# Packing the half-seen key tiles of the even query blocks two to a column, in an attention stage ahead of a routed feed-forward on one Trainium2 core

## The chip, the cores and the metric

The kernel runs on one core of one Trainium2 chip. The metric is device time in microseconds (us); lower is better. Its time before is the median of three runs, 455.78 us (454.82 to 455.80). The profile comes from one further execution, whose own time is 456.63 us and whose span, from the first to the last instruction, is 454.9 us. The granted TensorE clock was 0.996 of full speed over that span.

Engines are named as in the profile: PE is TensorE (matmul), PEld its weight loads, DVE is VectorE, ACT is ScalarE, POOL is GpSimd, SP is SyncE, which here issues DMAs.

## The reference, cut to what matters

```python
# attention: 8 batches x 8 heads, 576 positions, head size 64
block_i, block_j = pos[:, None] // 64, pos[None, :] // 64
scores = np.where(block_i >= block_j, q @ k.T / sqrt(64), -1e9)
attn = softmax(scores)                 # over the keys
x = attn @ v                           # [8, 576, 512] over all heads
# then a top-1 mixture of experts: 8 experts, relu(x @ w1[e]) @ w2[e], times a probability
```

A query block of 64 positions sees all keys of its own block and of the earlier ones. There are 9 query blocks, 0 to 8. A softmax does not change when one number is subtracted from all scores of a query, whatever the number.

## The kernel before, in words

**The work.** 64 heads are taken as 32 pairs. One pass of the loop at line 973 (a *round*, `it` from -2 to 31) works on up to four pairs at once: `a = it + 2` is being transposed (its q and k come in and are turned), `c = it + 1` gets its maxima and its first score segments, `e = it` gets its last score segments and its product with V, and `x = it - 1` is normalised and written to DRAM rows for the second stage. A feed-forward stage over 128-row tiles of tokens follows after round 31. A planner (`at`, `run`) strews small routing steps over the rounds 9 to 31, mostly on DVE.

**Scores.** They stand transposed: 128 keys in the partitions, queries in the columns. Key tile `j` holds key blocks `2j` and `2j + 1`; tile 4 holds block 8 alone. Both heads of a pair lie in one PSUM tile `[128, 2, 512]`, two banks. `SEGS` (line 411) lists four *segments*, each a list of (key tile, first query, number of queries, column). Tile 0 has 576 queries, tile 1 has 448, then 320, 192 and 64: 1600 columns for each head. A segment takes three steps: `products` (line 646) multiplies K by Q in fp32, one matmul for each head, 64 rows of the array each, and each of these shows as two passes in the profile; `less` (line 654) subtracts from each query its maximum, as a bf16 matmul of ones with a diagonal that holds minus the maximum; `expo` (line 663) takes the exponential on ACT from PSUM into `prob`.

**Half-seen tiles.** Query block `2j` sees only the first half of key tile `j`. `corners` (line 671) lets POOL overwrite the other half of these 64 columns with zeros, four memsets for each pair.

**Maxima.** `top` (line 573) forms scores once more in bf16 with queries in the partitions, into a PSUM tile of the same ring, and DVE reduces them. `top` job 2 covers the low query blocks, job 1 (`mid_maxima`, line 627) the middle ones and also block 0, job 0 (`high_maxima`, line 633) the high ones. From the maxima, `low_shift` on POOL (blocks 1 to 6), the end of `high_maxima` on DVE (blocks 7 and 8) and `first_shift` on DVE (block 0, line 617, two instructions, one for each head) write the diagonals. For pair 0 they stand in `diag0`; for all the other pairs there is one tile, `diag1`, `[128, 9, 64]`, written anew for each pair. `mid_maxima(i)` calls `first_shift(i)` for `i > 1`.

**V.** `av` (line 678) multiplies `prob` (64 queries as weights, 128 keys as rows) by `vt`, V with a column of ones, 50 matmuls of 65 columns for a pair.

**The order in a round from 1 to 29** (lines 1100 to 1223), as written; the order is kept, and each engine takes its own instructions strictly in it. A wait is put in by itself wherever an instruction reads what an earlier one in the written order wrote, or overwrites what an earlier one read:

1. `norm(x)` on DVE;
2. `mid_maxima(c, 0)`: PE scores, DVE reduce, POOL exchange, `first_shift(c)` on DVE;
3. segments 3 and 2 of pair `e`;
4. `turns` and `turned_in`: PE transposes of pair `a`, ACT copies into `plb`;
5. `low_shift(c)`, `high_maxima(c, 1)`, then on POOL `halves_in` (a copy into `qh`) and one corner;
6. products of segments 0 and 1 of pair `c`; `tails` (PE transposes, ACT copies); `top(a, 2, 1)`; small POOL copies and a cast;
7. `less` and `expo` of segments 0 and 1 of pair `c`, three corners, `low_exchange(a)`;
8. `av(e, ...)` and the normalisation of its last rows.

PSUM: three tiles `s0`, `s1`, `s2` for scores and maxima, reached through `ring`, whose last two entries change places after each round, and two banks `g0`, `g1` for transposes and `av`.

Of the kernel before, what the change touches and what calls it, by code (L numbers as in the profile page):

```python
# [16 lines left out]
def kernel(  # L17
# [11 lines left out]
    nc = tc.nc  # L29
    F32 = mybir.dt.float32  # L30
# [15 lines left out]
    P = 128  # L46
# [352 lines left out]
    def slots(inv, tok_g, tok_s):  # L399
# [4 lines left out]
        if tok_s is not None:  # L404
# [13 lines left out]
    def place(j, q0):  # L418
        for s, parts in enumerate(SEGS):
# [18 lines left out]
    with tc.manual_schedule():  # L438
# [223 lines left out]

        def expo(i, ps, s):
            p = prob[i % 2]
            w = sum(x[2] for x in SEGS[s])
            nc.scalar.activation(p[:, :, SEG0[s]:SEG0[s] + w], ps[:, :, 0:w],  # L666
                                 func=AF.Exp, scale=scale_attn)
            if s < 2:
                corners(i, s)

        def corners(i, s):
            p = prob[i % 2]
            for (j, a, n, c) in SEGS[s]:
                if j < 4 and a == 128 * j:
                    cc = SEG0[s] + c
                    nc.gpsimd.memset(p[64:128, :, cc:cc + 64], 0.0)  # L676

        def av(i, g, m):
# [9 lines left out]
            for h in range(2):  # L688
                for j in range(m + 1):
                    for e in range(2):  # L690
                        c = place(j, 128 * m + 64 * e)
                        nc.tensor.matmul(g[rows(e), o + 65 * h:o + 65 * h + 65],  # L692
                                         lhsT=p[:, h, c:c + 64], rhs=t[:, j, h, :],
                                         start=(j == 0), stop=(j == m))
# [278 lines left out]
        for it in range(-2, NPR):  # L973
# [56 lines left out]
            def tails():  # L1030

                tail = nat[:, 8].rearrange("p h d -> p (h d)") if on_a else None
                if on_x:
                    if it < NPR - 2:
                        g0, g1 = gx = g_tile(0), g_tile(1)
                    else:
                        ps = seg_tile(1 if on_c else 0)
                        gx = ps[:, 0, :], ps[:, 1, :]
                        g1 = gx[1]
# [43 lines left out]
            if it == -2:  # L1083
# [5 lines left out]
                top(0, 2, 1)  # L1089
                low_exchange(0)  # L1090
                weights(2)
                mid_maxima(0, 2)
# [3 lines left out]
                products(0, opened, 0, 1)  # L1096
                high_maxima(0, 1)
# [9 lines left out]
            if it == 0:  # L1107
                segment(3, 1)
                mid_maxima(c, 0)
                turns()  # L1110
                segment(2, 2)
            elif on_e:
# [3 lines left out]
                segment(3, 1)  # L1116
                segment(2, 2)
# [18 lines left out]
            if on_e:  # L1136
                corners(e, 2)
            run(it, "begin")
            if on_c and not on_e:
                ps0, ps1 = opened, seg_tile(2)  # L1140
                for z in range(2):
                    products(c, ps1, 1, z)
                top(a, 2, 1)
            if on_c and on_e:
                ps0, ps1 = seg_tile(0), seg_tile(2)
# [3 lines left out]
                products(c, ps0, 0, 1)  # L1149
            g1 = tails()  # L1150
            if on_e and on_a:
                top(a, 2, 1)
# [12 lines left out]
            if on_c:  # L1165
                for z, ps in enumerate((ps0, ps1)):
                    less(c, ps, z, 0)
                    less(c, ps, z, 1)
# [53 lines left out]
            if on_e:  # L1222
                ring[1:] = ring[:0:-1]
# [182 lines left out]
```

## Time and profile before

| | |
|---|---|
| median of 3 runs | 455.78 us |
| the profiled execution: its own time / its span | 456.63 / 454.9 us |
| PE busy | 429.3 us, 94% of the span |
| weight loads (PEld) busy | 338.4 us, 74% |
| DVE busy | 316.4 us, 70% |
| POOL busy | 295.5 us, 65% |
| ACT busy | 271.5 us, 60% |

A row of the timeline gives the start and the length of a group in us, then engine, line, operation, what it writes and reads with the shapes, the number of instructions (x), and in square brackets how long the engine had been idle before and what ended the wait. For a matmul the first shape is rows times columns of the array that it uses, the second rows times moving columns. A round begins with the PE rows of line 583.

### The profile page before, as it was taken

Reading aid. Unit: us, or ns where it says so; the run is one execution under the profiler, and the core shown is the slowest. Engines: PE = TensorE matmul, PEld = TensorE weight load, DVE = VectorE, ACT = ScalarE, POOL = GpSimd, SP = SyncE. Lnnn points to the kernel's source line nnn. Section 1 sums busy time; section 2 is a strip of 40 time slices with the busy share of each in tenths; the row PEclk is TensorE's granted clock in tenths of the full one; section 3 lists DMA queues with packets and bytes.
Section 4 is the critical chain, followed back from the end, with each engine's and each line's share of the span. In section 5 each row is a group of like instructions: output and inputs, shape, how many; then the busy total and the mean of one; then the engine's idle time right before and its main releaser. Section 6 shows DMA issues by size and latency. Waiting matters only on the chain. (4 is left out here: it accounts for less than half of the span.)

```text
span 454.9 us, 19769 instructions
## 1 busy us (share of the span) xinstructions
PE 429.3 (94%) x7780; PEld 338.4 (74%) x7802; DVE 316.4 (70%) x843; ACT 271.5 (60%) x573; POOL 295.5 (65%) x700
## 2 busy tenths in 40 slices
PE   7899899999999999899999999999999999999994
PEld 5688688878787877788778887786776676766772
DVE  4777667768778788887899998866865873333322
ACT  3856666766567757775777576454554553553552
POOL 4556466657556666887566788654877767667652
PEclk8999999999999999999999999999999999999999
DMA  7999799899999987999889998857545545555551
GB/s 153 187 164 173 138 177 184 157 186 171 184 171 171 170 167 149 194 157 180 172 167 178 163 192 145 143 107 161 139 131 154 143 124 155 146 123 156 138 122 66
DMA packets 169887, 71.18 MB, mean 156 GB/s; under 512 B 151424, under 2 KB 158080, under 8 KB 169792
## 3 DMA queue, kind: packets, MB, share of 16 engines
q1 hardware_dynamic: 154640, 38.05, 43.3%
q0 software_dynamic: 13952, 31.52, 34.4%
q8 instruction: 65, 1.06, 1.0%
q10 hardware_dynamic: 1200, 0.30, 0.3%
q14 instruction: 30, 0.25, 0.2%
HBM read 67.18 MB, written 14.97 MB: 181 GB/s over the span
## 5 line engine op out<-in xcount | busy, mean ns | idle before, releaser
L666 ACT ACTIVATE prob<-ps_s 128x640 f32<-128x640 f32 (+2 forms) x128 | 103.7, 839 | 44.1 <-PE ps_s L659 42.9
L594 DVE TENSOR_REDUCE mx<-ps_m 128x2 f32<-128x640 f32 (+2 forms) x96 | 100.3, 1044 | 17.5 <-PE ps_m L589 6.4
L650 PE MATMUL ps_s<-plb 64*128 64x320 f32 (+4 forms) x768 | 104.9, 394 | 1.2 <-DVE mx L597 0.9
L650 PEld LDWEIGHTS ps_s<-plb 64*128 64x128 f32 x768 | 69.2, 188 | 22.5 <-issue 11.1
L692 PE MATMUL g<-vt,prob 128*64 128x65 f32 x2560 | 81.1, 222 | 0.5 <-issue 0.4
L692 PEld LDWEIGHTS g<-vt,prob 128*64 128x64 f32 x2560 | 77.9, 138 | 1.0 <-issue 0.9
L827 ACT ACTIVATE hT<-ps_h 128x512 bf16<-128x512 f32 x76 | 43.9, 596 | 42.5 <-PE ps_h L823 28.4
L838 PE MATMUL ps_o<-w_bf,hT 128*128 x282 | 67.1, 379 | 1.4 <-issue 0.3
L838 PEld LDWEIGHTS <-hT 128*128 128x128 bf16 x304 | 28.0, 98 | 27.9 <-issue 0.3
L804 DVE COPY natb<-w_bf 128x4096 bf16 x20 | 24.7, 1236 | 30.9 <-PE ps_h L823 23.7
L841 ACT ACTIVATE o_sb<-ps_o,share 128x512 f32<-128x512 f32 x37 | 25.4, 687 | 29.5 <-PE ps_o L838 12.0
L804 DVE COPY plb<-w_bf 128x4096 bf16 x20 | 24.7, 1234 | 23.3 <-PE ps_h L823 13.7
L823 PEld LDWEIGHTS <-plb 128*128 128x128 bf16 x608 | 35.4, 98 | 7.0 <-issue 2.9
L823 PEld LDWEIGHTS <-natb 128*128 128x128 bf16 x608 | 35.4, 98 | 7.0 <-issue 2.3
L659 PE MATMUL ps_s<-diag,ones 64*128 64x448 bf16 (+1 forms) x372 | 36.7, 274 | 1.1 <-DVE diag L613 0.6
L63 POOL DMA_DIRECT2D w_bf<-in_moe_w_dram x56 | 34.1, 608 | 1.5 <-DMA x_rows<-xb 0.4
L1023 ACT COPY plb<-g 128x512 f32<-128x512 f32 x62 | 33.2, 593 | 1.2 <-PE g L987 1.2
L607 POOL COPY mx<-mx 64x2 f32<-64x2 f32 x64 | 11.7, 183 | 33.7 <-DVE mx L594 32.2
L676 POOL MEMSET prob<- 64x128 f32 x128 | 24.3, 205 | 13.1 <-ACT prob L666 7.6
L847 POOL DMA_INDIRECT out_dram<-o_sb,tok2s x17 | 19.0, 1117 | 20.0 <-ACT o_sb L841 10.9
L568 PE MATMUL ps_m<-kh,qh 64*128 64x320 bf16 (+2 forms) x192 | 25.7, 309 | 3.3 <-POOL qh L1028 1.2
L684 PEld LDWEIGHTS g<-vt,prob 128*64 128x64 f32 x640 | 21.4, 137 | 9.7 <-ACT xT L720 4.6
(291 smaller groups left out, 803.7 us busy)
## 6 DMA issues: line engine op xcount, KB each, us to landing
w_bf<-in_moe_w_dram POOLq DMA_DIRECT2D x48, 256.0 KB
vt<-in_v_dram SPq DMA_DIRECT2D x64, 128.0 KB
natb<-in_k_dram SPq DMA_DIRECT2D x63, 128.0 KB
natb<-in_q_dram SPq DMA_DIRECT2D x63, 128.0 KB
w_bf<-in_moe_w_dram POOLq DMA_DIRECT2D x8, 512.0 KB
x_rows<-w_bf SPq DMA_DIRECT2D x13, 256.0 KB
natb<-in_k_dram SPq DMA_DIRECT2D x32, 32.0 KB
vt<-in_v_dram SPq DMA_DIRECT2D x32, 32.0 KB
```

The source lines that it names most:

```text
L63: nc.gpsimd.dma_start(out=dst[:, e * WE:(e + 1) * WE].rearrange("p (k f) -> p k f", k=n)[:, r:r + m, :], in_=view[e][:, r:r + m, :])
L568: nc.tensor.matmul(ps[:, h, c:c + w], lhsT=qh[rows(h), 64 * b:64 * b + 128], rhs=kh[rows(h), 0:w], start=True, stop=m is None)
L594: nc.vector.reduce_max(mx[:, 7:12:4] if job == 0 else mx[:, b:b + 2], ps[:, :, 0:w], axis=AX)
L650: nc.tensor.matmul(ps[:, h, c:c + n], lhsT=pls[i][rows(h), S + 128 * j:S + 128 * j + 128], rhs=pls[i][rows(h), a:a + n], start=part == 0, ...
L659: nc.tensor.matmul(ps[:, h, c:c + n], lhsT=ones[rows(h), :], rhs=diag[rows(h), a // 64:(a + n) // 64, :], start=False, stop=part == len(SE ...
L666: nc.scalar.activation(p[:, :, SEG0[s]:SEG0[s] + w], ps[:, :, 0:w], func=AF.Exp, scale=scale_attn)
L692: nc.tensor.matmul(g[rows(e), o + 65 * h:o + 65 * h + 65], lhsT=p[:, h, c:c + 64], rhs=t[:, j, h, :], start=(j == 0), stop=(j == m))
L804: nc.vector.tensor_copy(w, w1_bf[:, bass.ds(off, WE)])
L823: nc.tensor.matmul(ps_h[:, f, :], lhsT=w[:, f0 + ko * F:f0 + ko * F + 2 * P - 1:2], rhs=xb[:, ko * P:(ko + 1) * P], start=(ko == 0), stop= ...
L827: nc.scalar.activation(hT[:, half * 4:half * 4 + 4, :], ps_h, func=AF.Relu)
L838: nc.tensor.matmul(ps_o, lhsT=hT[:, fo, :], rhs=w2_bf[:, bass.ds(woff + fo * Dm, Dm)], start=(fo == 0), stop=(fo == FO - 1))
L1023: nc.scalar.copy(pl[:, w * S:w * S + 512], pw[w])
```

## The change: what it does, and the diff

The half-seen tiles leave `SEGS`. Each of the four even blocks 0, 2, 4, 6 now has its own 64-key by 64-query piece, and two pieces share 64 columns: blocks 0 and 4 in one place (block 0 in partitions 0 to 63, block 4 in 64 to 127), blocks 2 and 6 in another. There are 1472 columns for each head, in three segments of 512, 512 and 448; the last one holds all four pieces. `products_halves` and `less_halves` make the pieces with matmuls of 64 rows by 64 columns of the array. The corners go; instead POOL copies the half of V that belongs to each piece into `vh`, a tile whose other half stays zero (`halves_v`, two copies for each pair), and `av` takes `vh` for the diagonal tile of an even block. The last segment of `e` is made in one go at step 3, with `s1`; maxima of steps 5 and 6 go to `s2`, segment 1 of pair `c` to `s1`, and the ring stays as it is after round 0.

```diff
-    SEGS = [[(1, 128, 448, 0), (4, 512, 64, 448)],
-            [(0, 0, 256, 0), (3, 384, 192, 256)],
-            [(2, 256, 320, 0)],
-            [(0, 256, 320, 0)]]
-    SEG0 = [448, 0, 960, 1280]
-    WP = 1600
+    SEGS = [[(0, 64, 512, 0)],
+            [(1, 192, 384, 0), (3, 448, 128, 384)],
+            [(2, 320, 256, 0), (4, 512, 64, 384)]]
+    HALVES = [(0, 0, 256), (4, 1, 256), (2, 0, 320), (6, 1, 320)]
+    SEG0 = [0, 512, 1024]
+    WP = 1472
...
+        vh = const([P, 4, 2, D + 1], F32, "vh")
+        nc.gpsimd.memset(vh, 0.0)
+        for z in range(2):
+            nc.gpsimd.memset(vh[64 * z:64 * z + 64, 2 * z:2 * z + 2, :, D:D + 1], 1.0)
...
+        def products_halves(i, ps):
+            for b, z, c in HALVES:
+                for h in range(2):
+                    nc.tensor.matmul(ps[rows(z), h, c:c + 64],
+                                     lhsT=pls[i][rows(h), S + 64 * b:S + 64 * b + 64],
+                                     rhs=pls[i][rows(h), 64 * b:64 * b + 64],
+                                     start=False, stop=False)
+
+        def less_halves(i, ps):
+            diag = diag1 if i else diag0
+            for b, z, c in HALVES:
+                for h in range(2):
+                    nc.tensor.matmul(ps[rows(z), h, c:c + 64], lhsT=ones[rows(h), 0:64],
+                                     rhs=diag[rows(h), b, :], start=False, stop=False)
...
-        def corners(i, s):
...
+        def halves_v(i):
+            for z in range(2):
+                nc.gpsimd.tensor_copy(vh[rows(z), 2 * z:2 * z + 2, :, 0:D],
+                                      vt[i % 2][rows(0), 2 * z:2 * z + 2, :, 0:D])
...
-                                         lhsT=p[:, h, c:c + 64], rhs=t[:, j, h, :],
+                                         lhsT=p[:, h, c:c + 64],
+                                         rhs=(t if e or j < m else vh)[:, j, h, :],
...
-            def segment(s, where):
+            def segment(where):
                 ps = seg_tile(where)
-                products(e, ps, s, 0)
-                less(e, ps, s, 0)
-                expo(e, ps, s)
+                for z in range(2):
+                    products(e, ps, 2, z)
+                products_halves(e, ps)
+                less_halves(e, ps)
+                for z in range(2):
+                    less(e, ps, 2, z)
+                expo(e, ps, 2)
...
                 if on_c:
                     mid_maxima(c, 0)
                 run(it, "mid")
-                segment(3, 1)
-                segment(2, 2)
+                segment(1)
                 if on_a:
                     turns()
...
-                    high_maxima(c, 1)
+                    high_maxima(c, 2)
...
-                corners(e, 2)
+                halves_v(e)
...
-                ps0, ps1 = seg_tile(0), seg_tile(2)
+                ps0, ps1 = seg_tile(0), seg_tile(1)
...
-                top(a, 2, 1)
+                top(a, 2, 2)
```

On PE, at step 3 of a round in the middle of the stage, before the change: two segments of pair `e`, products (line 650) and subtraction (line 659) of each, with no wait but the first. `ps_s` is the score tile, `plb` holds q and k, `diag` the diagonals.

```order
L650 MATMUL ps_s<-plb 128x320 [waits Activation_49]
L650 MATMUL ps_s<-plb 128x320
L659 LDWEIGHTS ones
L659 MATMUL ps_s<-diag,ones 128x320
L659 LDWEIGHTS ones
L659 MATMUL ps_s<-diag,ones 128x320
L650 MATMUL ps_s<-plb 128x320 x2
L659 LDWEIGHTS ones
L659 MATMUL ps_s<-diag,ones 128x320
L659 LDWEIGHTS ones
L659 MATMUL ps_s<-diag,ones 128x320
```

On PE at the same place now (line 657 is `products`, 673 `products_halves`, 682 `less_halves`):

```order
L657 MATMUL ps_s<-plb 128x256 [waits Activation_49]
L657 MATMUL ps_s<-plb 128x256
L657 MATMUL ps_s<-plb 128x64 x2
L673 MATMUL ps_s<-plb 64x64 x8
L682 LDWEIGHTS ones
L682 MATMUL ps_s<-diag,ones 64x64 [waits DVE_49]
L682 LDWEIGHTS ones
L682 MATMUL ps_s<-diag,ones 64x64 [waits DVE_49]
L682 LDWEIGHTS ones
L682 MATMUL ps_s<-diag,ones 64x64
```

One segment stands where two stood, eight small products and eight small subtractions are in it, and the first two subtractions, those of block 0, carry a wait for DVE each. In the built program the two counts that they wait for are those of the two instructions of line 627 (`first_shift`) that DVE runs for pair `c` in the same round.

On POOL, from step 5 to step 6, before (613 is `low_shift`, 1028 `halves_in`, 676 a corner, 1068 to 1072 `tails_in`):

```order
L613 TENSOR_TENSOR diag<-negi,mx 128x384 [waits PE_49,Pool_49]
L1028 CAST qh<-plb 128x512 [waits PE_49,Activation_49]
L676 MEMSET prob_148 64x2x64 [waits Pool_49]
L1068 CAST kh<-plb 128x64 [waits Activation_49,Pool_49]
L1069 CAST qh<-plb 128x64 [waits Activation_49]
L1072 CAST qh<-plb 128x2x64
```

On POOL at the same place now:

```order
L620 TENSOR_TENSOR diag<-negi,mx 128x384 [waits PE_49,Pool_49]
L1051 CAST qh<-plb 128x512 [waits PE_49,Activation_49]
L693 COPY vh<-vt_149 64x4x64 [waits DMAHW5_49,DMAHW4_49]
L693 COPY vh<-vt_149 64x4x64 [waits Pool_49]
L1091 CAST kh<-plb 128x64 [waits Activation_49,Pool_49]
L1092 CAST qh<-plb 128x64 [waits Activation_49]
L1095 CAST qh<-plb 128x2x64
```

Two copies stand where one memset stood; the other three memsets, later in the round between the cast and `low_exchange`, are gone.

More of the change, by code (lines that the diff above doesn't have):

```diff
@@ L1036, in tails @@
                     else:
[L1037 removed]
+                        ps = seg_tile(2 if on_c else 0)
                         gx = ps[:, 0, :], ps[:, 1, :]
@@ L1088 @@
                 load_ends(2)
-                top(0, 2, 1)
+                top(0, 2, 2)
                 low_exchange(0)
                 weights(2)
-                mid_maxima(0, 2)
+                mid_maxima(0, 1)
                 low_shift(0)
@@ L1095 @@
                 products(0, opened, 0, 0)
-                products(0, opened, 0, 1)
-                high_maxima(0, 1)
+                high_maxima(0, 2)
                 continue
@@ L1107 @@
             if it == 0:
-                segment(3, 1)
+                segment(2)
                 mid_maxima(c, 0)
                 turns()
-                segment(2, 2)
+                ring[1:] = ring[:0:-1]
             elif on_e:
@@ L1148 @@
                     products(c, ps1, 1, z)
-                products(c, ps0, 0, 1)
             g1 = tails()
             if on_e and on_a:
-                top(a, 2, 1)
+                top(a, 2, 2)
             if on_a:
@@ L1166 @@
                 for z, ps in enumerate((ps0, ps1)):
-                    less(c, ps, z, 0)
-                    less(c, ps, z, 1)
+                    for y in range(len(SEGS[z])):
+                        less(c, ps, z, y)
                     expo(c, ps, z)
```

18 lines of the change are left out of this document (5 added, 13 removed).

## The prediction

> **What bounds the kernel now.** I read the page first (PE busy in 94% of the span), then the busy time by windows, then the timeline of one whole round with all engines, and last the same few rows of every other round. The windows, with the length in us, then busy time of PE, PEld, DVE, ACT and POOL, then granted clock, DMA share and GB/s:
>
> ```profile
> 23.53:280.26 256.73, 248.53 (x5419) 204.50 (x5416) 206.76 (x557) 172.69 (x393) 171.79 (x536) 1.00 0.93 169
> 49.47:61.09 11.62, 10.28 (x220) 7.96 (x217) 7.46 (x20) 6.05 (x13) 7.38 (x25) 1.00 0.65 132
> 78.12:86.63 8.51, 8.41 (x188) 7.03 (x185) 6.32 (x16) 5.94 (x13) 5.36 (x17) 1.00 0.87 147
> ```
>
> The rounds 1 to 28 take 256.73 us and PE works in 248.53 of them. The third row is round 7, a plain one: 8.41 of 8.51 us. So the attention stage is bound by PE's instruction stream; whatever lengthens that stream or halts it is paid at once. The chain that ended last lies in the feed-forward stage, which the change does not touch. The plain round, from its timeline:
>
> ```profile
> 78.12 0.23 PE L583 MATMUL ps_m<-kh,qh 64*128 64x64 bf16 x4
> 78.41 0.70 PE L650 MATMUL ps_s<-plb 64*128 64x320 f32 x4
> 78.94 1.08 DVE L594 TENSOR_REDUCE mx<-ps_m 128x2 f32<-128x896 f32 x1
> 79.62 0.30 PE L659 MATMUL ps_s<-diag,ones 64*128 64x320 bf16 x2
> 79.76 0.66 PE L987 MATMUL g<-id_f,natb 64*128 64x64 f32 x16
> 80.25 0.38 PE L568 MATMUL ps_m<-kh,qh 64*128 64x512 bf16 x2
> 80.26 0.45 DVE L620 TENSOR_TENSOR diag<-negi,mx 64x64 bf16<-64x64 f32 x2
> 80.47 1.84 PE L650 MATMUL ps_s<-plb 64*128 64x448 f32 x16
> 80.62 1.07 ACT L1023 COPY plb<-g 128x512 f32<-128x512 f32 x2
> 80.74 1.23 DVE L594 TENSOR_REDUCE mx<-ps_m 128x2 f32<-128x1024 f32 x1
> 81.76 0.61 POOL L1028 CAST qh<-plb 128x512 bf16<-128x512 f32 x1
> 82.52 0.30 PE L568 MATMUL ps_m<-kh,qh 64*128 64x320 bf16 x2
> 82.53 0.29 DVE L613 TENSOR_TENSOR diag<-negi,mx 128x128 bf16<-128x128 f32 x1
> 82.87 0.59 PE L659 MATMUL ps_s<-diag,ones 64*128 64x448 bf16 x8
> 83.56 0.80 PE L684 MATMUL g<-vt,prob 128*64 128x65 f32 x20
> 84.20 2.50 PE L692 MATMUL g<-vt,prob 128*64 128x65 f32 x80
> 86.63 0.23 PE L583 MATMUL ps_m<-kh,qh 64*128 64x64 bf16 x4
> ```
>
> Three times matter below. S is the start of the segments of pair `e` (78.41). F is the end of `first_shift(c)` on DVE (80.26 + 0.45 = 80.71), so F − S = 2.30. V is the start of `av` (83.56), V − S = 5.15. Now the segments of `e` read nothing that DVE makes in this round: they end at 79.76, 0.95 us before F, and `first_shift` hurts nobody, since its block is subtracted only at 82.87.
>
> **The change part by part.** *The new wait.* Block 0 now lies in the last segment, which PE makes right after the scores of `mid_maxima(c)`. `less_halves(e)` reads block 0 of `diag1`; `first_shift(c)`, written ahead of it, has just overwritten that block with the shift of pair `c`, and both pairs share the one tile for `c` from 2 on. (The result bears it, since any shift does.) So PE stands at the first small subtraction until F, in the rounds 1 to 30. Its price: PE gets there at S plus the products, 0.54 us for 320 columns (half of the 1.35 from 78.41 to 79.76, less 0.14 for the subtraction, 79.62 to 79.76), plus 0.05 for one more part, 0.10 for a drain (below) and about 0.25 for the pieces: S + 0.9. F is at S + 2.30. PE stands for 1.4 us, and behind it in its queue stands everything else of the round: the rest of the segment, `turns`, the scores of `high_maxima`, products, `tails`, `top`, `av`. DVE waits for those `high_maxima` scores, so it idles too.
>
> How the rest follows F, in us after F: 0.05 until PE wakes (82.53 + 0.29 to 82.87 shows it for `diag1`); 0.11 for eight small subtractions (four such bf16 matmuls take 78.12 to about 78.19); 0.10 for a drain; 0.13 for the last 320 columns (79.62 to 79.76); so `turns` starts at F + 0.39. From `turns` to V are 3.80 now (79.76 to 83.56); segments 0 and 1 get 64 columns more and one part less, between 0 and 0.13, I take 0.04. V comes at F + 4.23, S + 6.53 in this round, 1.38 later than now.
>
> What else could be late by then: DVE's reduce for `high_maxima` starts when its scores are there, F + 0.39 + 0.49 + 0.38 + 0.1 = F + 1.36; to the end of its diagonal it needs 2.08 (80.74 to 82.82), so F + 3.44, and PE reaches that subtraction at F + 0.39 + 3.15 = F + 3.54. On ACT one exponential of 896 columns ends near F + 1.5, the copies of line 1023 near F + 2.5, POOL's `qh` near F + 3.15, and `top` wants it at F + 3.19. All tie, none adds.
>
> *The drains.* An array shape that changes costs a gap. The last six pairs of `av` passes ahead of line 583:
>
> ```profile
> 86.18 0.52 PE L692 MATMUL g<-vt,prob 128*64 128x65 f32 x12
> ```
>
> With 222 ns for one, the last pair starts at 86.48, and pairs follow each other by 0.06; line 583, which uses 64 rows by 128 columns, starts 0.15 after it, so 0.09 goes to the change of shape. The pieces add two such changes a round: the first is hidden by the wait, the second is the 0.10 above. The Trainium skill (TensorEngine Tiling (Array Packing), Key Properties) says that a changed tiling mode drains the engine, and gives no price; the row agrees, and a sum that let the pieces change shape for nothing would come out 29 × 0.10 = 2.9 us lower.
>
> *Can PE go on behind the wait?* Round 19 shows:
>
> ```profile
> 187.72 0.70 PE L650 MATMUL ps_s<-plb 64*128 64x320 f32 x4
> 189.25 0.48 DVE L620 TENSOR_TENSOR diag<-negi,mx 64x64 bf16<-64x64 f32 x2
> 191.77 0.71 DVE L613 TENSOR_TENSOR diag<-negi,mx 128x128 bf16<-128x128 f32 x1
> 193.01 0.31 PE L568 MATMUL ps_m<-kh,qh 64*128 64x320 bf16 x2 [1.02 <-POOL qh L1028]
> 193.80 0.39 PE L684 MATMUL g<-vt,prob 128*64 128x65 f32 x6
> ```
>
> The diagonal was ready at 192.48, and the subtractions that need only it stood behind line 568 until after 193.01. PE passed nothing forward. The Trainium skill (TensorE: Matmul & The Clock Gate, Part 3, The mechanism) says that matmuls start and end in strict order and only weight loads are pulled ahead; the round agrees, and by a freer order the whole sum below would vanish.
>
> *ACT and POOL.*
>
> ```profile
> L666 ACT ACTIVATE prob<-ps_s 128x640 f32<-128x640 f32 x64 | 45.0, 704 | 41.4 <-PE ps_s L659 40.2 <-POOL sm L163 0.3
> L666 ACT ACTIVATE prob<-ps_s 128x1024 f32<-128x1024 f32 x32 | 32.9, 1030 | 2.7 <-PE ps_s L659 2.7
> L676 POOL MEMSET prob<- 64x128 f32 x128 | 24.3, 205 | 13.1 <-ACT prob L666 7.6
> L1028 POOL CAST qh<-plb 128x512 bf16<-128x512 f32 x30 | 18.3, 610 | 3.8 <-ACT plb L1023 3.2
> ```
>
> ACT loses two exponentials of 704 ns a round and gets one of about 0.9 us, with 128 columns more in another; it waits 40.2 us for PE ahead of these already, so the saving is worth nothing. POOL loses four memsets (0.82 us) and gets two copies of 64 × 256 elements. Nothing like them is in the trace; between 0.2 (a memset) and 0.6 each (the cast of twice the length), I take 0.4. They follow the `qh` cast, near F + 3.2, and end by F + 4.4 at the worst; `av` needs `vh` after its ten first pairs, F + 4.9. Without that cover, with POOL a microsecond late, they could hold `av` by half a microsecond; the gone memsets make POOL earlier by about as much.
>
> *Fewer columns.* In V's products and in `turns` nothing changes. Without the wait the last segment would take about 1.28 us (0.59 products, two drains 0.20, pieces 0.25, subtractions 0.24) instead of 1.35: this saving the wait eats.
>
> *The sum over rounds.* The same three times, in three further rounds:
>
> ```profile
> 96.73 0.70 PE L650 MATMUL ps_s<-plb 64*128 64x320 f32 x4
> 98.27 0.45 DVE L620 TENSOR_TENSOR diag<-negi,mx 64x64 bf16<-64x64 f32 x2
> 101.89 0.51 PE L684 MATMUL g<-vt,prob 128*64 128x65 f32 x10 [0.17 <-ACT xT L720]
> ...
> 160.01 0.70 PE L650 MATMUL ps_s<-plb 64*128 64x320 f32 x4
> 162.33 0.45 DVE L620 TENSOR_TENSOR diag<-negi,mx 64x64 bf16<-64x64 f32 x2
> 165.59 0.63 PE L684 MATMUL g<-vt,prob 128*64 128x65 f32 x14
> ...
> 49.76 0.70 PE L650 MATMUL ps_s<-plb 64*128 64x320 f32 x4
> 50.42 0.72 POOL L515 CAST w_bf<-x 128x640 bf16<-128x640 f32 x1 [3.30 <-DMA x_rows<-w_bf]
> 53.59 0.45 DVE L620 TENSOR_TENSOR diag<-negi,mx 64x64 bf16<-64x64 f32 x2
> 56.81 0.39 PE L684 MATMUL g<-vt,prob 128*64 128x65 f32 x6
> ```
>
> Each round grows by (F − S) + 4.23 − (V − S). Thirteen rounds are like round 7, with F − S from 2.12 to 2.31: mean 1.32, together 17.2. Eight are like round 9, where other PE work ahead of S let DVE catch up (F − S = 1.99, V − S = 5.16): 1.05 each, 8.4. In five, DVE is late with routing steps, as in round 16 (2.77 and 5.58: 1.42); part of that work slides into the new hole, so 0.6 to 1.4, together 5.8. In rounds 19 and 28 POOL held PE already: 2.01 + 4.23 − 6.08 = 0.16, together 0.4. In round 4 a DMA held POOL for 3.30 us and DVE behind it (F − S = 4.28, V − S = 7.05); three longer rounds give that DMA some 4 us, so I let its wait go: 2.30 + 4.23 − 7.05 = −0.5 (+1.5 if it stays). Round 0 about 0.2, round 30 nothing (DVE was later there). Sum +31.5 us. The profiled execution took 456.63, 0.85 over the median; on the median, 455.78 + 31.5 = 487.
>
> **The rivals.** *The wait costs little* and the kernel gets faster. That holds if `first_shift` is done when PE comes, that is if F − S is under 0.9. Then 21 rounds win 0.07 us each, perhaps 0.13 if the pieces run faster than I took: about 454. Every round shows F − S of 1.98 or more, and the order shows the wait. *The longer rounds give more back*: DMA's share is 0.93 in these rounds and POOL and DVE are late in nine; if all waits but the plain ones dissolve, only the 21 rounds pay (25.6) and the other eight win some 0.5 each: 455.78 + 22 = 478. Against it: these engines wait on PE in nearly all rounds, and a wait that is not on PE's path gives nothing back. That the change leaves its work out can't be: the order shows the pieces and the wait.
>
> **How the numbers follow.** Forecast 0.87, give-back 0.09, the cheap wait 0.04. The forecast's own bounds: 0.1 us either way on the 0.39 and 0.04 in 27 rounds, 2.7 each way, round 4 up by 2, POOL and DMA waits down by 3: 481 to 493. The range reaches toward the second rival: 480 to 494. A measurement here tells 0.3% from nothing. Slower 0.96; the cheap wait divides into faster 0.03 and same 0.01.
>
> **What would show it.** Right: PE rows of the small subtractions (line 682) with about 1.4 us of idle time ended by DVE line 627 in nearly every round, a plain round of 9.9 us, and DVE idle ahead of the 1024-element reduce. Also PE's busy time near its old value with the span 31 us longer, and the clock still 1.00 (round 4, with 1.3 us of idle PE, kept it). Wrong: line 682 without a wait, or `av` later than F + 4.3, which would mean that ACT, POOL or DVE had taken over behind the wait.

## The result, and the profile after

The kernel after the change takes 491.62 us (median of 4 runs, 488.60 to 495.99); the kernel before took 455.79 us beside it (454.82 to 456.00). The ratio is 1.076, interval 1.072 to 1.080: slower, 4.6 us above the predicted 487 and inside the range 480 to 494.

The profiled execution is the longest of the four, 495.99 us with a span of 494.2 us, and was a disturbed one, such as all ratios here leave out: from the start of round 30 to its end it took 172.4 us, where a second profile of the same kernel has 163.0, and so only its attention stage is compared here, which agrees with that second profile within 0.2 us.

The windows of after: the rounds 1 to 29, then round 7 alone (columns as in the prediction).

```profile
24.68:321.78 297.10, 269.65 (x6135) 218.41 (x6132) 224.22 (x578) 167.41 (x378) 181.29 (x496) 1.00 0.79 150
85.24:95.17 9.93, 8.87 (x206) 7.18 (x202) 6.54 (x16) 5.56 (x12) 5.79 (x17) 1.00 0.92 172
```

The rounds 1 to 29 took 265.74 us before (from 23.53 to 289.27), so they grew by 31.4 us, and the plain round by 1.42. PE works 8.87 of 9.93 us in it, where it worked 8.41 of 8.51. Round 7 in the timeline of after:

```profile
85.53 0.76 PE L657 MATMUL ps_s<-plb 64*128 64x256 f32 x8
86.22 0.46 PE L673 MATMUL ps_s<-plb 64*64 64x64 f32 x16
87.37 0.47 DVE L627 TENSOR_TENSOR diag<-negi,mx 64x64 bf16<-64x64 f32 x2
87.64 0.50 PE L682 MATMUL ps_s<-diag,ones 64*64 64x64 bf16 x8 [0.96 <-DVE diag L627]
88.22 0.69 PE L1006 MATMUL g<-id_f,natb 64*128 64x64 f32 x16
88.75 0.38 PE L575 MATMUL ps_m<-kh,qh 64*128 64x512 bf16 x2
89.17 1.23 DVE L601 TENSOR_REDUCE mx<-ps_m 128x2 f32<-128x1024 f32 x1 [1.33 <-PE ps_m L575]
90.95 0.84 POOL L693 COPY vh<-vt 64x256 f32<-64x256 f32 x2
90.96 0.53 DVE L620 TENSOR_TENSOR diag<-negi,mx 128x128 bf16<-128x128 f32 x1
91.54 0.61 PE L666 MATMUL ps_s<-diag,ones 64*128 64x512 bf16 x6
91.85 0.21 ACT L739 COPY w_bf<-g 64x64 f32<-64x64 f32 x1
92.11 0.80 PE L702 MATMUL g<-vt,prob 128*64 128x65 f32 x20
```

With the names of the prediction: S is 85.53, F is 87.37 + 0.47 = 87.84, V is 92.11. PE has done the small products (line 673) and stands; the first small subtraction starts 0.05 after the first of the two instructions of line 627 has ended, and the rest 0.05 after the second. `turns` (line 1006) starts at F + 0.38 and `av` at F + 4.27. DVE then idles 1.33 us ahead of its 1024-element reduce, because the scores for it (line 575) stand behind PE's wait. Over the whole run, the list of waits of after, PE's row and DVE's (total us, times, longest):

```profile
PE ps_s L682 <- DVE diag L627: 25.2, 30, 1.3
DVE mx L601 <- PE ps_m L575: 35.6, 31, 1.4
```

Thirty rounds have the wait, and no other wait on PE comes near it.

### The profile page after: what moved, and what is told of

It is laid out like the page before. It is cut to its first block, busy times and chain, and to the rows that moved or that the text cites. A ratio compares the mean times of both kernels' runs of the same rounds, so it can differ in the third digit from the quotient of the medians.

```text
span 494.2 us, 20741 instructions
## 1 busy us (share of the span) xinstructions
PE 445.6 (90%) x8356; PEld 347.7 (70%) x8378; DVE 325.5 (66%) x843; ACT 258.8 (52%) x541; POOL 297.3 (60%) x639
## 4 chain that ended last, share of the span: by engine, by line
PE 56%; DVE 20%; issue 10%; POOL 6%; DMA 4%; ACT 2%; POOLq 1%; DVEq 0%; ACTq 0%
PE g L710 12%; PE ps_s L657 12%; DVE mx L601 7%; PE ps_h L842 5%; PE ps_s L666 5%; PE g L702 4%; PE ps_o L857 3%; PE g L1006 3%; DMA out_dram<-o_sb,tok2s 3%; POOL out_dram L866 3%; PE ps_m L575 3%; DVE diag L627 3%; DVE x L551 2%; PE g L776 2%; PE g L731 2%
## 5 line engine op out<-in xcount | busy, mean ns | idle before, releaser
L688 ACT ACTIVATE prob<-ps_s 128x1024 f32<-128x1024 f32 (+1 forms) x96 | 91.4, 989 | 98.1 <-PE ps_s L666 98.1
L657 PE MATMUL ps_s<-plb 64*128 64x512 f32 (+4 forms) x640 | 87.5, 399 | 1.4 <-DVE mx L606 0.8
L657 PEld LDWEIGHTS ps_s<-plb 64*128 64x128 f32 x640 | 61.9, 189 | 27.1 <-ACT prob L688 7.9
L710 PEld LDWEIGHTS g<-vt,prob 128*64 128x64 f32 x2048 | 77.9, 138 | 1.3 <-issue 1.2
L710 PE MATMUL g<-vh,prob 128*64 128x65 f32 x512 | 58.3, 222 | 0.3 <-ACT prob L688 0.3
L710 PEld LDWEIGHTS g<-vh,prob 128*64 128x64 f32 x512 | 45.1, 138 | 0.4 <-issue 0.4
L682 PE MATMUL ps_s<-diag,ones 64*64 64x64 bf16 x248 | 13.4, 199 | 27.1 <-DVE diag L627 25.2
L1051 POOL CAST qh<-plb 128x512 bf16<-128x512 f32 x30 | 18.3, 611 | 28.7 <-ACT plb L1046 27.1
L620 POOL TENSOR_TENSOR diag<-negi,mx 128x384 bf16<-128x384 f32 x31 | 25.7, 828 | 15.8 <-PE ps_s L666 15.4
L682 PEld LDWEIGHTS <-ones 64*64 64x64 bf16 x256 | 10.8, 104 | 33.5 <-issue 29.1
```

The costliest lines, as they stand in the source:

```text
L620: eng.tensor_tensor((diag1 if i else diag0)[:, b:b + n, :], negi[:, None, :].to_broadcast([P, n, 64]), mxs[i][:, b:b + n, None].to_broadca ...
L657: nc.tensor.matmul(ps[:, h, c:c + n], lhsT=pls[i][rows(h), S + 128 * j:S + 128 * j + 128], rhs=pls[i][rows(h), a:a + n], start=part == 0, ...
L710: nc.tensor.matmul(g[rows(e), o + 65 * h:o + 65 * h + 65], lhsT=p[:, h, c:c + 64], rhs=(t if e or j < m else vh)[:, j, h, :], start=(j == ...
```

## The experiments

They ran in four batches, the second on another chip than the other three. The kernel before took 450.66, 456.23, 454.98 and 454.44 us in them, and each ratio is to the runs of before in its own batch. "The stage" below is the time from the start of round 1 to the start of round 30, 265.74 us for before in the prediction's profile.

**The kernel after once more**, unchanged, as a mark for the others of its batch.

> The changed kernel once more, unchanged, on the chip and in the company of the other three: 487 to 492 by both theories; it shows how far the 5 us by which the profiled execution lay over the forecast belong to the feed-forward stage of that one execution (its attention stage alone was 32.5 us longer than before).

It took 484.69 us against 450.66, ratio 1.075 (1.070 to 1.079), the stage 297.25 us, the plain round 9.93. That is less than the 487 to 492 expected, but the kernel before is faster in this batch too, and the stage is the same within 0.2 us: the cost is there again.

**Block 0 in tiles of its own.** The shift of block 0 goes to one tile for each parity of the pair; `less_halves(e)` then reads what no instruction of this round writes.

```diff
+        own0 = [const([P, 64], BF16, f"own{i}") for i in range(2)]
...
-                    (diag1 if i else diag0)[rows(h), 0, :], negi[rows(0)],
+                    own0[i % 2][rows(h)], negi[rows(0)],
...
-                                     rhs=diag[rows(h), b, :], start=False, stop=False)
+                                     rhs=diag[rows(h), b, :] if b else own0[i % 2][rows(h)],
+                                     start=False, stop=False)
```

> The changed kernel, with the shift of block 0 in a tile of its own for each parity of the pair, so that the small subtraction of pair e no longer reads what first_shift(c) has just written. Theory W (the wait on first_shift is the whole loss): the wait at the small subtractions is gone from all rounds, a plain round takes 8.4 to 8.5 us, and the time is about 454 us (452 to 457). Rival P (the pieces themselves cost it: eight small products, eight small subtractions and two changes of array shape in each round): the time stays above 480.

Measured: 458.46 us, ratio 1.017 (1.013 to 1.020). Round 7 of its timeline (each line number is one above after's here):

```profile
78.85 0.76 PE L658 MATMUL ps_s<-plb 64*128 64x256 f32 x8
79.55 0.46 PE L674 MATMUL ps_s<-plb 64*64 64x64 f32 x16
79.83 0.20 PE L683 MATMUL ps_s<-own,ones 64*64 64x64 bf16 x2
80.15 0.69 PE L1008 MATMUL g<-id_f,natb 64*128 64x64 f32 x16
80.69 0.45 DVE L628 TENSOR_TENSOR own<-negi,mx 64x64 bf16<-64x64 f32 x2
82.87 0.85 POOL L695 COPY vh<-vt 64x256 f32<-64x256 f32 x2
82.97 0.44 DVE L621 TENSOR_TENSOR diag<-negi,mx 128x128 bf16<-128x128 f32 x1
84.03 0.80 PE L704 MATMUL g<-vt,prob 128*64 128x65 f32 x20
```

PE goes from the small products to the subtractions at S + 0.98, 0.86 us ahead of line 628, and reaches `turns` at S + 1.30; after had 2.69 there, before 1.35. With nothing else changed, 26 of after's 34 us are gone. This is the wait, and it is the shared tile that makes it. What stays is 1.7%, although the plain round is back at 8.54 us. Neither theory had that: theory W put this kernel at about 454, no slower than the kernel before. It was measured again in a later batch:

> The kernel with block 0 in its own tiles, once more and beside the next one, since its 1.7% over before came from one chip. If that is its true place, the ratio is 1.013 to 1.020 again, with plain rounds of 8.54 us; if it was the course of DMAs on that chip, it is anywhere from 1.00 to 1.01.

462.98 us, ratio 1.019 (1.014 to 1.023). So the packing without its wait is slower than the kernel before, in both batches.

**The wait alone, in the kernel before.** Two matmuls with weights of zero read block 0 of `diag1` ahead of the subtraction of segment 2. They add nothing to the scores, but PE has to wait for `first_shift(c)` there.

```diff
+        nil = const([P, P], BF16, "nil")
+        nc.vector.memset(nil, 0.0)
...
             def segment(s, where):
                 ps = seg_tile(where)
                 products(e, ps, s, 0)
+                if s == 2 and e:
+                    for h in range(2):
+                        nc.tensor.matmul(ps[:, h, 0:64], lhsT=nil[rows(h), :],
+                                         rhs=diag1[rows(h), 0, :], start=False, stop=False)
                 less(e, ps, s, 0)
```

> The kernel before, with nothing of the change but a wait: ahead of the subtraction of segment 2, two matmuls of 64 columns with weights of zero read block 0 of the diagonal tile, so PE stands there until first_shift of the next pair is done. Theory W: V comes at F + 0.05 + 0.03 + 0.14 + 3.80 = F + 4.02, 0.21 less than forecast for the change because no drain and fewer subtractions follow, so 25 us more: about 481 (476 to 486). Rival P: two more small matmuls, under 2 us: 455 to 458.

484.38 us, ratio 1.076 (1.071 to 1.080): the whole loss, without one piece being packed. That is 33.7 us above the kernel before of its batch, where theory W had 25. The stage alone, 293.45 us, is 27.7 longer than in the prediction's profile, against 31.5 for after in this batch. The wait alone (33.7) and the packing without it (7.8) come to more than after's 34.0 us together; how they overlap is not shown. Round 7:

```profile
84.89 0.47 DVE L622 TENSOR_TENSOR diag<-negi,mx 64x64 bf16<-64x64 f32 x2
85.16 0.44 PE L1005 MATMUL ps_s<-diag,nil 64*128 64x64 bf16 x2 [0.74 <-DVE diag L622]
89.54 0.80 PE L686 MATMUL g<-vt,prob 128*64 128x65 f32 x20
```

F is 85.36 and V 89.54, F + 4.18 in this round and 4.09 in most plain ones, 0.18 less than in after, which has the drain, the pieces' subtractions and the longer products still behind F.

**The segment ahead of the middle maxima.** The rows read what the round before left in `diag1`, so the wait goes, and the order on PE is the price.

```diff
+                segment(1)
                 if on_c:
                     mid_maxima(c, 0)
                 run(it, "mid")
-                segment(1)
```

> The changed kernel with the last segment of pair e made ahead of mid_maxima(c), so that it reads block 0 before it is overwritten. Theory W with DVE's chain as the pace: no wait at the small subtractions, but the scores of mid_maxima start 1.26 us later; DVE has done norm by then and its chain to the diagonal takes 4.4 us from those scores, so av comes 6.23 us after the round's begin against 5.44 before: 0.8 us a round, about 476 (470 to 481). If only PE's stream counted: about 454. Rival P: above 480.

484.29 us, ratio 1.075 (1.071 to 1.080): no better, and 8 us over the 476 expected. Its round of 9.61 us, with PE, DVE and ACT (83.77 is the start of the scores of line 590):

```profile
82.36 0.87 PE L657 MATMUL ps_s<-plb 64*128 64x256 f32 x8
83.77 0.22 PE L590 MATMUL ps_m<-kh,qh 64*128 64x64 bf16 x4
84.25 1.09 DVE L601 TENSOR_REDUCE mx<-ps_m 128x2 f32<-128x896 f32 x1 [0.98 <-PE ps_m L596]
85.26 0.28 DVE L606 TENSOR_REDUCE mx<-ps_m 128x2 f32<-128x128 f32 x1
85.58 0.45 DVE L627 TENSOR_TENSOR diag<-negi,mx 64x64 bf16<-64x64 f32 x2
85.69 2.00 PE L657 MATMUL ps_s<-plb 64*128 64x512 f32 x12 [0.77 <-DVE mx L606]
86.05 1.23 DVE L601 TENSOR_REDUCE mx<-ps_m 128x2 f32<-128x1024 f32 x1
88.65 0.21 ACT L739 COPY w_bf<-g 64x64 f32<-64x64 f32 x1
88.91 0.80 PE L702 MATMUL g<-vt,prob 128*64 128x65 f32 x20
```

Now DVE stands for 0.98 us until the segment has passed, and from there on it works without a gap: reduce, line 627, reduce at once (86.05 is 0.02 after 86.03). PE's next products (85.69) wait 0.77 us for the short reduce of line 606, which ends at 85.54 and frees their score tile. Behind the products come the transposes of `tails` and ACT's copies of them, and `av` starts 0.05 after the last copy (88.65 + 0.21 = 88.86), at F + 2.88. In before `av` came at F + 2.85 (80.71 to 83.56), with the reduce 0.03 after F as well, and there too its weight loads wait for ACT's last copy:

```profile
79.94 0.28 DVE L599 TENSOR_REDUCE mx<-ps_m 128x2 f32<-128x128 f32 x1
83.31 0.21 ACT L720 COPY w_bf<-g 64x64 f32<-64x64 f32 x1
83.56 0.66 PEld L684 LDWEIGHTS g<-vt,prob 128*64 128x64 f32 x20 [0.36 <-ACT w_bf L720]
```

There the products (80.47) start 0.25 us after the reduce that frees their tile has ended (80.22), against 0.15 in the row above where they wait for it. So the chain of DVE's first two reduces, PE's products, `tails` and ACT's copies was within 0.1 us of PE's own stream in the plain round of before. DVE's second reduce and shift were level too: the shift ends at 82.82, and the subtraction behind it starts at 82.87.

The expected sum was too low in the price of a round: 0.8 us expected, 1.10 measured, in the short rounds as well (9.61 us in the rounds 5 and 9). `av` comes 6.55 us after the start of the segment, not 6.23: the scores start at 1.41 instead of 1.26, and `av` comes 0.77 after the end of the diagonal, where the sum had 0.57.

**Where the other 1.7% comes from: POOL's copies?** In own blocks DVE's last shift takes 0.44 us where it took 0.29, beside the copies into `vh`. Four kernels try this. *Copies early*: as own blocks, with the copies at the round's start.

```diff
+            if on_e:
+                halves_v(e)
             if it == 0:
                 segment(2)
...
-            if on_e:
-                halves_v(e)
             run(it, "begin")
```

> Block 0 has its own tile for each parity, and the two copies into vh now stand at the start of the round on POOL, which idles there for 1.8 us in a plain round, instead of between the qh cast and tails_in. Theory 1 (the copies run beside DVE's last shift and stretch it from 0.29 to 0.44 us, and in rounds where POOL is late they hold it for 0.84 more): the shift is back at 0.29, the diagonal at 4.70 after the first matmul instead of 4.85, the plain round 8.51, and the special rounds lose less: ratio 1.005 to 1.010 to before. Theory 2 (the loss of 1.7% is not POOL's: 64 more columns stand ahead of tails, and av waits for the copies of tails): av stays at 5.47, the plain round at 8.54, ratio 1.015 to 1.018.

468.37 us, ratio 1.025 (1.021 to 1.029): slower still. The shift is back at 0.29 and the diagonal at 4.72, but `av` stays at 5.47 to 5.49 in the plain rounds, as theory 2 said, whose ratio was still too low. The loss is in other rounds (round 2 takes 12.59 us) and ahead of round 1, which starts at 26.32 us, in own blocks at 23.63. POOL's waits and PE's:

```profile
POOL vh L695 <- DMA vt<-in_v_dram: 7.7, 2, 4.2
POOL vh L695 <- PE g L712: 4.7, 4, 2.3
```
```profile
PE ps_m L576 <- POOL qh L1053: 7.1, 4, 2.5
```

The copy needs V, which at the round's start has not always landed, and the `vh` of the pair before, which `av` still reads. POOL stands on it with the exchange, the shift and the `qh` cast queued behind, and PE's scores in turn stand for `qh`: 7.1 us, against 0.8 and 1.1 in the two profiles of own blocks. That way of hiding the copies costs more than the copies.

*The copies alone*, in the kernel before, into a tile that nobody reads; and four of them, with (0, 1, 0, 1) in place of range(2).

```diff
+        vh = const([P, 2, 2, D + 1], F32, "vh")
+        nc.gpsimd.memset(vh, 0.0)
...
             if on_e:
                 corners(e, 2)
+                for z in range(2):
+                    nc.gpsimd.tensor_copy(vh[rows(z), :, :, 0:D],
+                                          vt[e % 2][rows(0), 2 * z:2 * z + 2, :, 0:D])
```

> The kernel before with nothing changed but two more POOL copies of 64 x 256 elements of V, into a tile that nothing reads, behind the corner of segment 2. Theory 1: DVE's last shift grows from 0.29 to about 0.44 us, the diagonal comes at 4.85, av goes from 5.44 to about 5.5, the special rounds in which POOL is late grow by up to 0.8 us: ratio 1.008 to 1.015. Theory 2: av hangs on the copies of tails on ACT and has 0.1 us to spare, POOL has room: ratio 1.000 to 1.003.

> The kernel before with four such copies in place of the two, 1.6 us of POOL in each round. If POOL's time is what two copies cost, four cost more than twice as much (POOL has 3 us to spare in a plain round, less than 1 us between the qh cast and the kh cast): ratio 1.02 to 1.05, with the top job 2 scores waiting for POOL's casts in the plain rounds. If the 1.0% of two copies was the feed-forward stage and not POOL, the ratio stays near 1.01.

Two copies: 460.56 us, ratio 1.010 (1.006 to 1.014). Four, in the next batch: 471.18 us, 1.036 (1.031 to 1.041), more than three times as much. The plain round stays at 8.51 with two (the stage is 266.68 us, where before's two profiles have 265.74 and 267.39), and the last shift stays at 0.29 there, because the copies begin 0.22 us behind it: the ratio is theory 1's, but not by way of the plain rounds; with four, some plain rounds reach 8.60 and the stage 278.05. PE's wait for POOL's `qh` cast, with two copies and with four (the kernel before has 1.2 and 1.6 us in its two profiles):

```profile
PE ps_m L570 <- POOL qh L1030: 2.3, 3, 1.0
```
```profile
PE ps_m L570 <- POOL qh L1030: 4.7, 4, 1.7
```

So POOL has room for the two copies in a plain round and none for two more in the rounds where it is late. Where the 1.0% of two copies lies the one profile does not show, since its stage is not longer.

*Own blocks without the copies.*

> Block 0 in its own tiles, and the two POOL copies into vh are left out: the diagonal products of the even blocks read zeros in place of V. If the copies make the 1.7% (two copies in the unchanged kernel made 1.0%, though its plain rounds stayed at 8.51 us), this comes to 1.002 to 1.008 of before, with DVE's last shift back at 0.29 us and the short waits for diagonals in the rounds 16 and 24 to 27 gone. If the columns ahead of tails and the smaller array shapes make it, it stays at 1.013 to 1.018.

```diff
-            if on_e:
-                halves_v(e)
             run(it, "begin")
```

464.05 us, ratio 1.014 (1.009 to 1.020), where own blocks with them had 1.019 (1.014 to 1.023) in the same batch. So the copies' share of the loss is about a quarter by these ratios, and most of it is still there without them; the intervals overlap, so even that share is not certain.

**Is it PE's stream?** *Part of segment 1 behind tails*, with the copies early:

```diff
                 products(c, ps0, 0, 0)
-                for z in range(2):
-                    products(c, ps1, 1, z)
+                products(c, ps1, 1, 0)
             g1 = tails()
+            if on_c and on_e:
+                products(c, ps1, 1, 1)
```

> As with the copies early and block 0 in its own tiles; besides, the last part of segment 1 (128 columns for each head) is made behind tails instead of ahead of it. In the run with own blocks av began 0.05 after the last ACT copy of tails in the plain rounds, though its PE work was done 0.05 to 0.1 before. By theory 2 (64 more columns stand ahead of tails) tails starts 0.27 earlier, av is then bound by PE alone and comes at 5.36 to 5.40, and the kernel is 1.5 to 3 us faster than with the copies early alone, at best level with before. By theory 1 nothing hangs on tails: as long as with the copies early, within 1 us.

`av` comes at 5.28 to 5.34 in the plain rounds, and the shortest round is 8.35 us, 0.16 below the kernel before, a little better than theory 2 had it. The kernel takes 469.58 us, 1.026 (1.021 to 1.031), no faster than with the copies early alone, where theory 2 had it 1.5 to 3 us faster. Its waits:

```profile
PE ps_m L576 <- POOL qh L1053: 6.1, 6, 1.8
PE g L1008 <- issue: 2.5, 2, 1.3
```

*The pieces left out*, with one subtraction of 128 columns for each head in their place:

```diff
-                products_halves(e, ps)
-                less_halves(e, ps)
+                for h in range(2):
+                    nc.tensor.matmul(ps[:, h, 256:384], lhsT=ones[rows(h), :],
+                                     rhs=(diag1 if e else diag0)[rows(h), 7:9, :],
+                                     start=False, stop=False)
```

> Block 0 in its own tiles, and the work on the half-seen pieces is left out of TensorE: their eight products and eight subtractions, with both changes of array shape, are replaced by one bf16 subtraction of 128 columns for each head, so the scores there are wrong. It gives the most that any cheaper packing could win. The 32 short passes, the drains and what replaces them stand for about 0.4 us a round between the start of the segment and turns (0.46 for the products' rows, 0.23 for the subtractions', partly beside others). Theory 1 (the attention stage is bound by PE's stream in the plain rounds, as the prediction says): turns at 1.2 instead of 1.58 after the first matmul, plain round 8.1 to 8.2, and 24 rounds give 8 to 10 us: 448 to 452 where the kernel before takes 455, ratio 0.985 to 0.995. Theory 2 (transfers bound the stage as soon as the rounds get shorter; a kernel with plain rounds of 8.35 was no faster than one with 8.54): plain rounds of 8.1 to 8.2 too, but more and longer waits for q, k, V or row transfers in other rounds, ratio 1.00 to 1.015.

457.39 us, ratio 1.006 (1.002 to 1.010). Round 7 (it starts at 79.92):

```profile
81.00 0.73 PE L1008 MATMUL g<-id_f,natb 64*128 64x64 f32 x16
81.74 0.28 DVE L607 TENSOR_REDUCE mx<-ps_m 128x2 f32<-128x128 f32 x1
82.05 0.45 DVE L628 TENSOR_TENSOR own<-negi,mx 64x64 bf16<-64x64 f32 x2
82.17 2.00 PE L658 MATMUL ps_s<-plb 64*128 64x512 f32 x12 [0.22 <-DVE mx L607]
82.53 1.23 DVE L602 TENSOR_REDUCE mx<-ps_m 128x2 f32<-128x1024 f32 x1
85.12 0.21 ACT L741 COPY w_bf<-g 64x64 f32<-64x64 f32 x1
85.38 0.34 PE L704 MATMUL g<-vt,prob 128*64 128x65 f32 x4
```

`turns` starts at 1.08 after the round's start, 0.56 earlier than before. PE then waits 0.22 for DVE's short reduce (its score tile is not free until 81.74 + 0.28 = 82.02), and `av` comes at 5.46, F + 2.88, 0.05 after ACT's last copy (85.33): the chain that the segment ahead of the middle maxima showed. This round takes 8.53 us, as before. Only the rounds in which DVE is early (F at 2.27) fall to 8.22, and there `av` comes at F + 2.88 as well. So theory 1 is wrong in a point that the prediction shared: taking 0.5 us out of PE's stream saves nothing in the plain rounds where DVE is level with it, and the most that any cheaper packing could win there is near nothing. Theory 2 has the ratio, but its plain rounds of 8.1 to 8.2 did not come. And the kernel as a whole is no faster than before: its list of waits has

```profile
PE g L712 <- issue: 2.7, 3, 1.4
PE ps_s L658 <- DVE mx L607: 2.4, 11, 0.2
PE g L1008 <- issue: 1.7, 1, 1.7
```

**The kernel before once more**, profiled in the second batch for comparison.

> The kernel before, unchanged, for a profile on the same chip as its neighbours. The plain round should be 8.51 us again, with segments of pair e to turns 1.35 and av at 5.44 after the first matmul of the round. The open point is the special rounds: with blocks of their own the kernel needed 458.5 us where before took 450.7, though its plain round was 8.54 against 8.51. If the loss there belongs to the packing, the rounds 10, 16, 18 and 28 are shorter here by about 0.4, 1.1, 0.2 and 1.7 us than in that run; if it is the course of DMAs on that chip, they are as long here, or other rounds are.

Ratio 0.999 to its neighbours (0.996 to 1.002). Its plain round is 8.51; its rounds 10, 16, 18 and 28 are 9.03, 10.29, 9.04 and 10.96 us, against 9.81, 11.29, 9.28 and 12.72 in the first profile of own blocks, as expected of a loss that belongs to the packing. But its own rounds 2, 8 and 15 are 0.8 to 0.9 longer than in the first profile of before, and in the second profile of own blocks the four rounds take 10.91, 10.19, 9.28 and 11.41. So long rounds wander from one execution to the next, here by up to 1.3 us, and these profiles do not show in which rounds it lies. One wait is new with the packing: POOL's copies stand for V's transfer, 3.7 us in all in the first profile of own blocks and 4.0 in the second. The stages of the profiled executions, before first, then own blocks again, without copies, without pieces:

```profile
22.80:290.19 267.39, 257.98 (x5612) 211.95 (x5609) 214.92 (x578) 179.06 (x407) 178.43 (x555) 1.00 0.91 167
```
```profile
24.26:295.79 271.53, 261.46 (x6135) 214.87 (x6132) 216.16 (x578) 167.59 (x378) 180.28 (x496) 1.00 0.91 164
```
```profile
24.93:295.64 270.71, 259.69 (x6133) 213.70 (x6132) 212.65 (x578) 167.74 (x378) 159.16 (x438) 1.00 0.92 165
```
```profile
22.97:291.44 268.47, 253.45 (x5496) 206.34 (x5494) 216.06 (x578) 168.22 (x378) 180.56 (x496) 0.99 0.90 166
```

All four move 164 to 167 GB/s in the stage, with the DMA share at 0.90 to 0.92. What the packing takes from PE is not to be seen: it has 523 more passes than before (6135 − 5612) and 3.5 us more busy time, for 128 fewer columns for each head. That the stage is held by its transfers as well, so that what a plain round gains a later one gives back, would fit the rates and the waits that turn up in other rounds each time; but the waits marked "issue", up to 1.8 us, have no releaser in the trace, and no run here changed the transfers. So the cause of the last 1.4 to 1.9% stays open.

No version beats the kernel before.

## Why the prediction was right

**The mechanism** was the wait that the order showed: taking it away brings back 26 of 34 us, putting it into the kernel before brings a loss as large (by the stage, 27.7 of 31.5 us).

**The sum by rounds**, measured as the period of each round in the profile after less that in the profile before:

| rounds | predicted | measured |
|---|---|---|
| 13 plain (1, 2, 3, 6, 7, 8, 14, 15, 20, 22, 23, 26, 27) | +17.2 | +17.2 |
| 8 short (5, 9, 11, 12, 13, 17, 21, 29) | +8.4 | +8.6 |
| 5 with DVE late (10, 16, 18, 24, 25) | +5.8 | +5.6 |
| 19 and 28 | +0.4 | +0.4 |
| 4 | −0.5 | −0.5 |
| 1 to 29 together | +31.3 | +31.4 |
| start of round 1 | +0.2 | +1.2 |

That these agree so well is in part chance. The step V − F came out as 4.27 in nearly all rounds instead of 4.23, which adds 1.1 us (in the rounds 5, 21, 25 and 29 it is 4.31 to 4.33, just past the F + 4.3 given as a sign of another engine behind the wait; which one adds the 0.04 there is not shown), and in the rounds 2, 11 and 15 waits of 0.3 to 0.7 us from the profile before were gone, which takes 1.4. Round 4 did lose its DMA wait: F is back at S + 2.31 there. The start of round 1 was mis-sized by 1 us; in the profiled executions of all kernels here it lies anywhere from 22.8 to 26.3 us, for the kernel before at 22.8 and 23.5.

**The 4.6 us by which the median lies above the forecast** are 1.0 from this (round 30 starts 32.5 us later instead of 31.5), 0.3 from rounding the forecast, and 3.3 that lie in no round. The medians differ by 35.8 us here and by 34.0 in the first batch of the experiments. From the start of round 30 to the end the profiles of all kernels have 162 to 172 us, so these 3.3 cannot be assigned.

**The small terms.** `turns` at F + 0.38 (0.39 predicted). DVE's reduce at F + 1.33 (1.36). The end of its last shift at F + 3.65 (3.44), because a copy into `vh` held the shift, 0.53 us instead of 0.29; the subtraction behind it starts at F + 3.70 (3.54). `av` still starts 0.05 after ACT's last copy (92.06), so no price of this shows there. The segment without its wait, in own blocks, 1.30 (1.28 predicted: the two drains, the pieces and their subtractions as a whole are right to 0.02). POOL's copies 0.84 us for the two (0.8), from F + 3.11 to F + 3.95. The idle time at line 682 reads 0.96 where the prediction said about 1.4: the row counts from the modelled end of the last small product, and PE wakes once for each head. The delay is right all the same: `turns` at S + 2.69 against 1.30 without the wait is 1.39.

**What failed** is not on the forecast's path but in its frame. "Whatever lengthens that stream or halts it is paid at once" held; that PE alone bounds the stage did not. PE's busy share of 99% in the plain round hid that a chain over DVE and ACT ended level with it: the reduce that frees the score tile ends 0.1 us before it would hold the products up, DVE's next reduce starts 0.03 after F, and `av` stands for ACT's copies of `tails`, 0.17 us in round 9. The Trainium skill (Perfetto Trace Analysis, Identifying the Most-Contended Engine) says that matmul busy time is not a good measure of how close a kernel is to the roofline; round 7 without the pieces is in line with that: PE reaches `turns` 0.5 us earlier than in own blocks, and the round takes the same 8.5 us. For the same reason the rival "the wait costs little", priced at 454, would have been wrong even with its condition met: own blocks met it and took 1.7 to 1.9% more than before, not 0.4% less.

## What to carry to other kernels

When an edit makes one engine read a buffer that another engine rewrites in the same round, look at the order for the count that the reader now waits for, and price the wait by everything that is queued behind the reader: here it cost 1.4 us in a plain round and 31 in all, and a second buffer of 64 columns took three quarters of the loss away. Before work is shaved off the busiest engine, leave that work out altogether in a kernel made for the purpose: here one such run showed that a plain round had nothing to win, because a chain over DVE and ACT ended at the same moment.

## What the runs showed of the hardware

**A DVE operation with two inputs beside a POOL copy.** The shift of line 620 takes 0.29 us by itself. Where a copy into `vh` starts up to 0.25 us ahead of it, the shift ends 0.54 us after the start of the copy, however early it was itself: 90.95 and 91.49 in round 7 of after, 82.87 and 83.41 in own blocks. Where the copy had begun longer ahead than that, or began after the shift, the shift took 0.29, except beside other POOL instructions. A copy that began 0.04 to 0.10 us behind the shift took 0.45 to 0.51 instead of 0.39. So the one that comes first holds the other off: the copy the shift for about 0.25 us, the shift the copy for up to 0.16. The Trainium skill (SBUF — State Buffer, Who interferes with whom) says that a DVE instruction with two SBUF inputs contends with a GpSimd instruction that reads SBUF, and that the port pair they share is an exclusive lock; these rows agree, and the time held is here less than the whole copy.

**Small pieces.** The 16 passes of 64 rows by 64 columns start at 79.55 in own blocks and the subtractions behind them at 79.83, 0.28 us. In round 7 of after they start in four groups of four, within 0.02 us in each group, 0.11 from the first group to the second and 0.06 after that, each pass shown as 0.22 to 0.27 long: four quarters of the array work side by side.
